# Eight output products per two steps for the last token pair, one accumulating DMA less, and output weights kept whole in DRAM

## The chip, the cores and the metric

The kernel runs on one core of one Trainium2 chip. The metric is the device time of one execution in microseconds (us). TensorE is called PE, its weight loads PEld, VectorE DVE, ScalarE ACT, GpSimd POOL and SyncE SP.

## The reference

```python
X = np.fft.rfft(x, axis=1)                      # x: 2 x 3008 x 256
Yr = Xr @ w_r - Xi @ w_i + b_r; Yi = Xr @ w_i + Xi @ w_r + b_i
Y = shrink(Yr, 0.01) + 1j * shrink(Yi, 0.01)
t = np.fft.irfft(Y, n=3008, axis=1).reshape(6016, 256)
h = t @ moe_w_in                                # 256 -> 2048
t = (h * clip(h + 3, 0, 6) / 6) @ moe_w_out     # 2048 -> 256
g, v = t @ moe2_w_gate, t @ moe2_w_val          # 256 -> 1536 each
out = (silu(g) * v) @ moe2_w_out                # 1536 -> 256
```

Everything is float32. A product of two float32 matrices is made of three fast matmuls: each operand is split into a high part and a rest (`hi`, `lo`), and low x high, high x high and high x low are added in one PSUM bank. "A product" below is such a group of three matmuls of a 128x128 weight block with up to 512 columns of tokens.

## The kernel before, in words

The 6016 tokens, kept transposed, form six **pairs** of two equal blocks: five pairs with 512 tokens per block and a last one with 448 (`pairs`, `halves`, L530 and L779). Three stages follow each other: the Fourier layer, the first feed-forward layer (`quad1`, L1003) and the second feed-forward layer, which the change touches (`quad`, L1280, and `last`, L1372). While `quad1` runs, `Convert2.steps` (L707) turns the float64 weights of the second layer into float32 parts, step by step, and writes one tile `Wd[f]` in DRAM for each of the 12 blocks f of 128 hidden units.

**A step of the second layer** is one pair p and one f: 72 steps. Its 2x2 block product (two token blocks, gate and value) is made with seven products in place of eight (`multiply`, numbers 1, 2, 7, 6, 4, 5 in the step and 3 in the next one), in the banks P, T and Q. P holds products 1, 6, 5 and 3 one after another; each partial result is copied out or added by ACT or DVE before the next product is added to it. P changes between two banks from step to step. Each step applies Silu twice (L1352, L1367) and multiplies gate and value (`times2`).

**The output products.** For two steps (f = 2k and 2k + 1) the output too is a 2x2 block product with seven products in place of eight. That needs sums of hidden units (`units`, four per k: T1 to T4, in SBUF) and of output weights (`out_sums`, `out_parts`, in the first pair). Three products of each k are made at once (`live`, into the banks `acc`); one of them takes T1, the other two sums that are ready in the next step. The other four wait (`later`): they are made in the steps of the **next** pair, two products per step, into one bank D. D begins with a copy of the first `acc` (`begin`, L1150), and `phase` reads it after steps 2, 5, 8 and 11. For them `part2` (L1140) splits units of two k at a time, 1024 columns on ACT (L1145) and DVE (L137), and `ask` (L1128) loads their weights (`chunk` from `Vd`). The last pair has no next pair: `last` makes its 24 waiting products, the last product 3 and two `live` products after all steps.

**Sums of units.** In an odd step T1 is added to T3 (L1306, `add_apart`: an accumulating DMA that POOL issues at L1254); T2 += T1 of the k before is a DVE instruction (`add_up`, L1251); T2 += T4 is another accumulating DMA. In the next even step DVE adds T2 to T3. Each instruction waits for the one whose result it reads.

**Weights.** Four slots hold the weights of a step: 14 blocks for the seven products and 2 or 4 output blocks, 1024 or 1152 KB per fetch (`fetch`, L854), issued on SP two steps ahead. A slot is free once the step after its own has used its output blocks. In the first pair `ask_out` (L1210) loads output weights for `out_sums`: as `Wd` holds them only as high part and rest, SP loads the one and POOL adds the other by an accumulating DMA. `out_parts` (L1238) writes the summed weights to `Vd` (512 KB) and `Wd`; in an odd step of the first pair SP meets those two writes, then the fetch of the odd step, then that of the next even step.

The order on each engine is the order of the calls; nothing reorders them (`manual_schedule`). Each queue works in order, and an instruction that waits holds up what is behind it.

Of the kernel before, what the change touches and what calls it, by code (L numbers as in the profile page):

```python
# [10 lines left out]
F32 = mybir.dt.float32  # L11
# [3 lines left out]
AF = mybir.ActivationFunctionType  # L15
# [67 lines left out]
def fourier_moe_kernel(ctx: ExitStack, tc: tile.TileContext, x, lin, bias, w1, w2, fwd1, inv2, fwd2,  # L83
# [17 lines left out]
    def one_bank(i, shape, name):  # L101
        return ps.tile(shape, F32, tag=f"pp{i % 5}", name=name, bufs=1)
# [593 lines left out]
    class Convert2(Convert):  # L696
# [10 lines left out]
        def steps(self):  # L707
            n = len(self.pieces)
            for i in range(4):
                self.load(i)  # L710
            yield
            self.scale(0)
            yield
            for i in range(n + 1):
                if i < n:
                    self.shift(i)
                if i > 0:
                    self.sign(i - 1, self.full_of(i - 1))
# [24 lines left out]
                yield  # L743

# [109 lines left out]
    def fetch(q):  # L854
        if q < len(stream):
            assert stream[q] in ready, (q, stream[q])
            slot[q] = free.pop(0)
            src = (Sd, Wd)[stream[q][0] - 1][stream[q][1]]
            c = src.shape[1] // 128
            if stream[q][0] == 2 and (stream[q][1] % 2 == 0 or q < len(quads1) + KF2):  # L860
                c = 16
            nc.sync.dma_start(slot[q][:, :c].bitcast(F32).rearrange("p a b -> p (a b)"), src[:, : c * 128])

    def side(k=1):
        for _ in range(k):
# [283 lines left out]

    def begin(p):  # L1150
        n = halves[p]
        D = C[p, 3] = C[p, 0] = one_bank(spot[0], [128, BLK], "D")
        a = acc.pop((p, 1))
        nc.scalar.copy(D[:, :n], a[:, :n])  # L1154
        c = C[p, "one"] = take("one")
        nc.scalar.copy(c[:, :n], a[:, :n])

    def later(p, i, half):
        m, kk = divmod(i, 3)
        n = halves[p]  # L1160
        (hi, lo), w = mid[p, i], mid[p, i, "w"]
        o = C[p, 3 * (m == 3)]
        wh, wl = w[:, 2 * half], w[:, 2 * half + 1]
        o, xh, xl = pairwise(o[:, :n]), woven(hi[:, half]), woven(lo[:, half])
        start = (p, "end") in C and i == 9 and not half
        nc.tensor.matmul(o, wl, xh, start=start, stop=False, skip_group_check=not start)  # L1166
        nc.tensor.matmul(o, wh, xh, start=False, stop=False, skip_group_check=not start)  # L1167
        nc.tensor.matmul(o, wh, xl, start=False, stop=True, skip_group_check=not start)

    def send_out(p, e, t, c, send=nc.sync):  # L1170
        n = halves[p]
# [2 lines left out]

    def phase(p, m):
        n = halves[p]
        D, one, three = C[p, 0][:, :n], C[p, "one"][:, :n], C[p, "three"][:, :n]
        if m == 0:
            nc.vector.tensor_tensor(out=one, in0=D, in1=one, op=ALU.subtract)
        elif m == 1:  # L1180
            nc.vector.tensor_tensor(out=three, in0=D, in1=three, op=ALU.add)
            send_out(p, 0, 1, three)
        elif m == 2:
            c = take("short")[:, :n]
            nc.scalar.copy(c, D)
            send_out(p, 1, 1, c)
            if (p, "end") in C:
                nc.vector.tensor_tensor(out=one, in0=D, in1=one, op=ALU.subtract)
        elif (p, "end") in C:
            nc.vector.tensor_tensor(out=one, in0=C[p, 3][:, :n], in1=one, op=ALU.add)  # L1190
            send_out(p, 1, 0, one)
# [46 lines left out]
    def out_parts(k):  # L1238
        g = G.pop(k)
        t = cv.tile([128, 4, 2, 128], F32R, tag="full", name="parts", bufs=2)  # L1240
        f = fourth[k] = cv.tile([128, 2, 128], F32R, tag="s4", name="s4", bufs=1)
        nc.scalar.copy(t[:, :, 0], g[:, :4])
        nc.scalar.copy(f[:, 0], g[:, 4])
        low(t[:, :, 1], g[:, :4], t[:, :, 0])
        low(f[:, 1], g[:, 4], f[:, 0])
        nc.sync.dma_start(Vd[:, :, k], t.bitcast(F32).rearrange("p m i c -> p m (i c)"))
        nc.sync.dma_start(Wd[2 * k + 1][:, 16 * 128 :], f.bitcast(F32).rearrange("p i c -> p (i c)"))

    def add_up(p, k, to, x):
        o = U(p, to, k)  # L1250
# [29 lines left out]
    def quad(q, before):  # L1280
# [84 lines left out]
        times2(U(p, ("T1", "T4")[odd], k), h0[:, :n], Q[:, :n], -1 if odd else 1)  # L1365
        todo.send()
        nc.scalar.activation(h1[:, :n], h1[:, :n], AF.Silu)  # L1367
        if f == NF - 1:
            begin(p)
        return p, k, odd, P, h1, product, n  # L1370

    def last(before):  # L1372
        p, k = before[:2]
        w = slot[F0 + len(quads2) - 1]
        order = (0, 1, 2, 3, 4, 5, 9, 6, 7, 8, 10, 11)
        C[p, "end"] = True
        C[p, 3] = one_bank(spot[0] + 4, [128, BLK], "E")

        def both(at):
            for half in range(2):  # L1380
                later(p, order[at], half)
            if at + 2 < 12:
                ask(p, order[at + 2])

        both(0)
        upper(before)
        part2(p, 1)
        x2 = halve(p, k, "T4")
        both(1)
        x3 = halve(p, k, "T2")  # L1390
        add_up(p, k, "T3", "T2")
        add_up(p, k, "T2", "T1")
        add_apart(p, k, "T4", "T2")
        part2(p, 2)
        live(p, 2, k, w[:, 14:16], x2)
        both(2)
        live(p, 3, k, w[:, 16:18], x3)
        corner(p)
        third(p)
        phase(p, 0)  # L1400
        part2(p, 3)
        for at in range(3, 12):
            both(at)
            if at + 1 < 12:
                part2(p, order[at + 1])
            if order[at] in (5, 8, 11):
                phase(p, order[at] // 3)

    lay_out()
    ask_out(0)  # L1410
# [2 lines left out]
    for q in range(len(quads2)):  # L1413
        if quads2[q][1] == 0 and quads2[q][0] + 1 < len(pairs):
            p = quads2[q][0] + 1
            todo.steps = iter(operands(len(pairs) + p, p, from_dram(len(pairs) + p, p)))
        before = quad(q, before)
    last(before)
    assert not pending


# [58 lines left out]
```

## Time and profile before

| | us |
|---|---|
| median of 3 runs (1171.15 to 1174.17) | 1174.11 |
| the profiled execution | 1175.45 |
| its span, first to last instruction | 1173.3 |

| engine | busy us, share of the span |
|---|---|
| PE | 1120.2 (95%) |
| PEld | 975.2 (83%) |
| DVE | 985.4 (84%) |
| ACT | 820.3 (70%) |
| POOL | 121.9 (10%) |

Mean granted TensorE clock: 0.985. Busy time is the time in which at least one instruction of the engine runs. Matmuls overlap in the trace: one of 512 columns is shown with 0.38 us, but the next begins sooner. In a timeline row the first number is the start, the second the duration; the bracket at the end tells how long the engine was idle before and what ended that. In a row of waits stand the total, the number of waits and the longest one. In a row of windows stand the stretch, its length, the busy time of PE, PEld, DVE, ACT and POOL (in brackets how many instructions), the granted clock, the DMA share and GB/s. The second layer runs from about 590 us on.

### The profile page before, as it was taken

Reading aid. Unit: us, or ns where it says so; the run is one execution under the profiler, and the core shown is the slowest. Engines: PE = TensorE matmul, PEld = TensorE weight load, DVE = VectorE, ACT = ScalarE, POOL = GpSimd, SP = SyncE. Lnnn points to the kernel's source line nnn. Section 1 sums busy time; section 2 is a strip of 40 time slices with the busy share of each in tenths; the row PEclk is TensorE's granted clock in tenths of the full one; section 3 lists DMA queues with packets and bytes.
Section 4 is the critical chain, followed back from the end, with each engine's and each line's share of the span. In section 5 each row is a group of like instructions: output and inputs, shape, how many; then the busy total and the mean of one; then the engine's idle time right before and its main releaser. Section 6 shows DMA issues by size and latency. Waiting matters only on the chain.

```text
span 1173.3 us, 20145 instructions
## 1 busy us (share of the span) xinstructions
PE 1120.2 (95%) x7362; PEld 975.2 (83%) x7362; DVE 985.4 (84%) x1720; ACT 820.3 (70%) x1506; POOL 121.9 (10%) x153
## 2 busy tenths in 40 slices
PE   8999999999999999999998788999999998999996
PEld 8999888788888888888997566887887887887885
DVE  6888888999999999999986676987887987887775
ACT  4777666787787888877876565676676776676573
POOL 3000018000000000000012211111111111111110
PEclk9999999999999999999999898999999999999998
DMA  7757337754645645645557878788688789679764
GB/s 299 283 178 230 95 96 240 259 195 163 210 157 173 227 162 168 225 144 179 194 144 211 247 233 269 219 279 276 196 272 280 221 244 310 188 242 289 229 176 131
DMA packets 94058, 250.32 MB, mean 213 GB/s; under 512 B 8836, under 2 KB 37796, under 8 KB 82504
## 3 DMA queue, kind: packets, MB, share of 16 engines
q1 hardware_dynamic: 78448, 222.61, 54.4%
q0 software_dynamic: 15360, 26.35, 11.8%
q8 instruction: 58, 0.95, 0.3%
q14 instruction: 40, 0.33, 0.1%
q10 hardware_dynamic: 152, 0.08, 0.0%
HBM read 186.48 MB, written 44.04 MB: 196 GB/s over the span
## 4 chain that ended last, share of the span: by engine, by line
PE 49%; issue 31%; DVE 7%; DMA 5%; POOL 4%; ACT 3%; ACTq 0%; POOLq 0%; DVEq 0%
PE acc L132 6%; PE acc L134 6%; PE acc L133 6%; POOL units L1254 4%; PE P L940 3%; PE P L942 3%; PE P L941 3%; DMA units<-units 2%; PE p L461 2%; PE p L367 2%; PE Tb L940 2%; PE Tb L941 1%; PE Tb L942 1%; PE p L417 1%; DVE r L988 1%
## 5 line engine op out<-in xcount | busy, mean ns | idle before, releaser
L617 ACT CAST gated<-r 128x512 fp32r<-128x512 f32 (+1 forms) x160 | 98.1, 613 | 64.7 <-DVE r L988 63.1
L1352 ACT ACTIVATE hv<-hv 128x512 f32<-128x512 f32 (+1 forms) x72 | 44.7, 621 | 127.6 <-DVE hv L1351 127.6
L137 DVE TENSOR_TENSOR gated<-r,gated 128x512 fp32r<-128x512 f32 (+1 forms) x160 | 108.0, 675 | 24.0 <-ACT gated L617 19.5
L132 PE MATMUL acc<-gated,w_o 128*128 128x512 f32 (+1 forms) x320 | 120.4, 376 | 0.0
L133 PE MATMUL acc<-gated,w_o 128*128 128x512 f32 (+1 forms) x320 | 119.6, 374 | 0.0
L134 PE MATMUL acc<-gated,w_o 128*128 128x512 f32 (+1 forms) x320 | 119.6, 374 | 0.0
L1254 POOL DMA_DIRECT2D units<-units x72 | 65.2, 1063 | 420.9 <-DVE hv L137 393.5
L940 PE MATMUL P<-xo,slot 128*128 128x512 f32 (+1 forms) x240 | 91.6, 382 | 5.4 <-DMA slot<-Wd 2.1
L984 ACT ACTIVATE r<-hold,consts 128x512 f32<-128x512 f32 (+1 forms) x120 | 85.5, 712 | 13.9 <-DVE hold L992 11.8
L942 PE MATMUL P<-xo,slot 128*128 128x512 f32 (+1 forms) x240 | 89.3, 372 | 0.0
L941 PE MATMUL P<-xo,slot 128*128 128x512 f32 (+1 forms) x240 | 89.3, 372 | 0.0
L988 DVE SCALAR_TENSOR_TENSOR r<-r,hold 128x512 f32<-128x512 f32 (+1 forms) x120 | 80.9, 674 | 2.6 <-ACT r L984 1.6
L1145 ACT CAST parts<-units 128x1024 fp32r<-128x1024 f32 (+1 forms) x72 | 74.2, 1032 | 5.2 <-PE D L1167 5.0
L1166 PE MATMUL D<-parts,chunk 128*128 128x512 f32 (+1 forms) x138 | 55.0, 399 | 17.6 <-ACT D L1154 7.3
L1270 ACT CAST live<-units 128x512 fp32r<-128x512 f32 (+1 forms) x108 | 63.7, 608 | 11.1 <-DVE units L1258 10.7
L132 PEld LDWEIGHTS acc<-gated,w_o 128*128 128x128 f32 x320 | 60.5, 189 | 7.0
L134 PEld LDWEIGHTS acc<-gated,w_o 128*128 128x128 f32 x320 | 60.5, 189 | 6.9
L133 PEld LDWEIGHTS acc<-gated,w_o 128*128 128x128 f32 x320 | 60.5, 189 | 6.7
L1251 DVE TENSOR_TENSOR units<-units 128x512 f32<-128x512 f32 (+1 forms) x72 | 48.6, 674 | 17.8 <-DMA units<-units 17.8
L137 DVE TENSOR_TENSOR parts<-units,parts 128x1024 fp32r<-128x1024 f32 (+1 forms) x36 | 43.3, 1202 | 21.9 <-ACT parts L1145 21.8
L1216 POOL DMA_DIRECT2D hv<-Wd x12 | 14.8, 1638 | 446.8 <-DMA hv<-Wd 419.1
L940 PEld LDWEIGHTS P<-xo,slot 128*128 128x128 f32 x240 | 45.4, 189 | 16.8 <-DVE hv L1364 4.5
(249 smaller groups left out, 3419.3 us busy)
## 6 DMA issues: line engine op xcount, KB each, us to landing
slot<-Wd SPq DMA_DIRECT2D x42, 1024.0 KB
slot<-Sd SPq DMA_DIRECT2D x40, 896.0 KB
slot<-Wd SPq DMA_DIRECT2D x30, 1152.0 KB
chunk<-Vd SPq DMA_DIRECT2D x72, 256.0 KB
st<-in_w SPq DMA_DIRECT2D x68, 256.0 KB
units<-units POOLq DMA_DIRECT2D x60, 256.0 KB, 6.3
Wd<-slot SPq DMA_DIRECT2D x12, 1152.0 KB
m<-in_fwd SPq DMA_DIRECT2D x12, 512.0 KB
```

The costliest lines, as they stand in the source:

```text
L132: nc.tensor.matmul(o, wl, xh, start=start, stop=False)
L133: nc.tensor.matmul(o, wh, xh, start=False, stop=False)
L134: nc.tensor.matmul(o, wh, xl, start=False, stop=stop)
L137: nc.vector.tensor_tensor(out=o, in0=full, in1=hi.bitcast(F32), op=ALU.subtract)
L617: nc.scalar.copy(hi[:, :n], g[:, :n])
L940: nc.tensor.matmul(o, wl, hi, start=start, stop=False, skip_group_check=not start)
L941: nc.tensor.matmul(o, wh, lo, start=False, stop=False, skip_group_check=not start)
L942: nc.tensor.matmul(o, wh, hi, start=False, stop=True, skip_group_check=not start)
L984: nc.scalar.activation(r[:, :n], x[:, :n], AF.Relu, bias=three)
L988: nc.vector.scalar_tensor_tensor(out=r[:, :n], in0=r[:, :n], scalar=6.0, in1=x[:, :n], op0=ALU.min, op1=ALU.mult)
L1145: nc.scalar.copy(hi, t[:, :, :n])
L1254: nc.gpsimd.dma_start(U(p, to, k), U(p, x, k), accum_op=ALU.add)
```

## The change

- The last pair makes its output products directly, all eight for two steps (four per step), and none of them waits: `last` goes, and `plain` takes the place of `quad` for f = 1 to 11 of the last pair and is called once more for the end. It still makes the waiting products of the pair before. Its P stays in one bank, as the other one holds the fourth output sum. The two values of a step are kept in two spots (`own`), and `share` multiplies those of the step before.
- T3 += T1 in odd steps is a DVE instruction (`add_up`) in place of an accumulating DMA; for the last pair no unit sums are made at all. 30 of 72 accumulating DMAs of L1254 are left.
- In the step f = 11 the copy from the first `acc` to D is issued after L1338's copy and so ahead of both Silu instructions; its second copy (`one`) stays behind them.
- The conversion also writes the full output weights to a new DRAM tile `Od`; `Wd[f]` has 20 blocks in place of 18 and is written by two DMAs. `ask_out` is one load of 256 KB from `Od`, without an accumulating DMA.
- A fetch of the last pair is two DMAs (16 blocks, and 2 blocks from the end of `Wd[f]`).

```diff
-    Wd = [dram.tile([128, SLOT * 128], F32, name=f"Wd{f}") for f in range(KF2)]
+    Wd = [dram.tile([128, 20 * 128], F32, name=f"Wd{f}") for f in range(KF2)]
+    Od = [dram.tile([128, 4, 128], F32, name=f"Od{k}") for k in range(KF2 // 2)]
...
                 O = full.pop((f, 2))
+                nc.sync.dma_start(Od[f // 2][:, f % 2 * 2 : f % 2 * 2 + 2], O)
...
-                nc.sync.dma_start(Wd[f], t.bitcast(F32).rearrange("p a b -> p (a b)"))
+                nc.sync.dma_start(Wd[f][:, : 16 * 128], t[:, : 16 * 128])
+                nc.sync.dma_start(Wd[f][:, 18 * 128 :], t[:, 16 * 128 :])
...
+            if stream[q][0] == 2 and p == len(pairs) - 1:
+                nc.sync.dma_start(to[:, 16 * 128 :], src[:, 18 * 128 :])
...
     def begin(p):
         n = halves[p]
-        D = C[p, 3] = C[p, 0] = one_bank(spot[0], [128, BLK], "D")
+        D = C[p, "D"] = one_bank(spot[0], [128, BLK], "D")
         a = acc.pop((p, 1))
+        C[p, "one"] = take("one")
         nc.scalar.copy(D[:, :n], a[:, :n])
-        c = C[p, "one"] = take("one")
-        nc.scalar.copy(c[:, :n], a[:, :n])
+        return lambda: nc.scalar.copy(C[p, "one"][:, :n], a[:, :n])
...
     def ask_out(k):
         F[k] = take("outs").rearrange("p (a b) -> p a b", b=128)
-        for i in range(2):
-            t = F[k][:, 2 * i : 2 * i + 2]
-            w = Wd[2 * k + i][:, 14 * 128 :].rearrange("p (e h c) -> p e h c", e=2, h=2)
-            nc.sync.dma_start(t, w[:, :, 0])
-            nc.gpsimd.dma_start(t, w[:, :, 1], accum_op=ALU.add)
+        nc.sync.dma_start(F[k], Od[k])
...
             x1 = halve(p, k, "T1")
-            add_apart(p, k, "T1", "T3")
+            add_up(p, k, "T1", "T3")
...
             fetch(F0 + q + ASK)
+            if f == NF - 1:
+                then = begin(p)
...
         if f == NF - 1:
-            begin(p)
+            then()
...
-    def last(before):
...
+    def plain(q, before):
...
+        if p is not None:
+            fetch(F0 + q + ASK)
...
+        last(Pb, 3)
+        s1 = take("own")
+        times2(s1[:, :n], hb[:, :n], Pb[:, :n], 1)
+        if p is not None:
+            later(old, i, 0)
+            later(old, i, 1)
+        x0 = parted(state["own"])
+        if p is None:
+            x1 = parted(s1)
+            for t, x in enumerate((x0, x1)):
+                for e in range(2):
+                    share(t, e, x)
...
+        product(P, 1, start=True)
+        nc.scalar.copy(Q[:, :n], P[:, :n])
+        x1 = parted(s1)
+        if i % 3 == 2:
+            phase(old, i // 3)
+        product(T, 7, start=True)
...
+        share(0, 0, x0)
+        product(Q, 2)
+        product(P, 6)
+        if i + 1 < NF:
+            part2(old, i + 1)
...
+        share(0, 1, x0)
+        product(T, 4)
...
+        share(1, 0, x1)
+        product(P, 5)
+        h1 = take("h")
+        nc.vector.tensor_tensor(out=h1[:, :n], in0=P[:, :n], in1=c7, op=ALU.add)
+        share(1, 1, x1)
+        free.append(slot.pop(F0 + q - 1))
+        state["own"] = take("own")
+        times2(state["own"][:, :n], h0[:, :n], Q[:, :n], 1)
+        nc.scalar.activation(h1[:, :n], h1[:, :n], AF.Silu)
```

`share` is one product (three matmuls) of a step's value, split by `parted` (a copy on ACT, a subtraction on DVE), with an output block of the slot. In the last call the fourth sum is copied out in two halves, one by DVE and SP's queue, one by ACT and ACT's queue.

## Rows read from the trace of the kernel before

**Rows 1.** Windows: one of the first layer, pairs 1, 4 and 5, the end.

```profile
225.00:590.00 365.00, 363.43 (x2375) 319.14 (x2374) 341.60 (x635) 292.14 (x519) 0.00 (x0) 1.00 0.53 182
...
722.50:807.50 85.00, 82.55 (x380) 71.16 (x380) 73.04 (x106) 59.75 (x102) 10.41 (x12) 1.00 0.83 256
...
981.30:1068.80 87.50, 84.23 (x381) 72.44 (x380) 72.45 (x106) 58.95 (x102) 10.44 (x12) 0.98 0.78 248
1068.80:1142.10 73.30, 69.01 (x339) 63.67 (x337) 55.59 (x85) 46.42 (x84) 10.47 (x12) 0.98 0.74 221
1142.10:1173.30 31.20, 20.47 (x81) 16.26 (x81) 18.14 (x22) 13.40 (x19) 0.86 (x1) 0.86 0.48 138
```

**Rows 2.** Windows: two stretches at half clock; two-step cycles of the first pair.

```profile
652.70:656.10 3.40, 3.16 (x7) 2.08 (x8) 3.27 (x9) 1.70 (x4) 0.00 (x0) 0.50 0.98 332
...
1144.20:1151.00 6.80, 5.76 (x17) 4.57 (x15) 4.89 (x8) 2.10 (x4) 0.00 (x0) 0.50 0.37 116
630.90:644.70 13.80, 11.55 (x53) 9.44 (x52) 11.10 (x22) 8.98 (x19) 3.49 (x4) 1.00 0.73 239
...
694.20:707.80 13.60, 11.14 (x49) 8.46 (x47) 11.81 (x22) 8.95 (x19) 1.74 (x2) 1.00 0.76 244
```

**Rows 3.** Waits of PE from 615 to 720 us (the first pair).

```profile
PE P L940 <- DMA slot<-Wd: 10.9, 5, 3.0
...
PE D L1166 <- DMA chunk<-Vd: 5.2, 1, 5.2
```

**Rows 4.** Waits from 720 to 1142 us (pairs 1 to 5).

```profile
DVE parts L137 <- ACT parts L1145: 20.2, 29, 2.0
...
DVE units L1251 <- DMA units<-units: 11.9, 5, 2.9
...
PE D L1166 <- ACT D L1154: 5.5, 4, 1.4
...
PE P L940 <- DVE hv L1364: 3.5, 5, 0.7
...
PE D L1166 <- DVE sums L1179: 2.3, 4, 0.8
PE P L940 <- DMA slot<-Wd: 2.1, 1, 2.1
PE D L1168 <- DVE lows L137: 2.1, 5, 0.4
```

**Rows 5.** DMA queues from 643 to 653 us, and one kind of issue.

```profile
q1 hardware_dynamic: 862, 2.08, 62.8%
q0 software_dynamic: 759, 0.67, 43.2%
...
units<-units POOLq DMA_DIRECT2D x2, 256.0 KB, 11.1
```

**Rows 6.** Timeline: DVE's additions L1251 in steps 1 and 2 of pair 3.

```profile
897.68 0.69 DVE L1251 TENSOR_TENSOR units<-units 128x512 f32<-128x512 f32 x1
...
907.59 0.69 DVE L1251 TENSOR_TENSOR units<-units 128x512 f32<-128x512 f32 x1 [2.52 <-DMA units<-units]
```

**Rows 7.** Timeline: matmuls of the last pair, its last step, and the end.

```profile
1124.77 0.38 PE L1166 MATMUL D<-parts,chunk 128*128 128x512 f32 x1
...
1125.41 0.35 PE L940 MATMUL Tb<-xo,slot 128*128 128x448 f32 x1
...
1125.60 0.35 PE L941 MATMUL Tb<-xo,slot 128*128 128x448 f32 x1
...
1140.97 0.35 PE L942 MATMUL P<-xo,slot 128*128 128x448 f32 x1
...
1141.47 0.61 DVE L1364 TENSOR_TENSOR hv<-P,cc 128x448 f32<-128x448 f32 x1
...
1142.12 0.58 ACT L1367 ACTIVATE hv<-hv 128x448 f32<-128x448 f32 x1
...
1169.72 0.62 DVE L1190 TENSOR_TENSOR sums<-E,sums 128x448 f32<-128x448 f32 x1 [1.12 <-PE E L1168]
```

More of the change, by code (lines that the diff above doesn't have):

```diff
@@ L858, in fetch @@
             src = (Sd, Wd)[stream[q][0] - 1][stream[q][1]]
[L859 to L862, printed above, removed]
+            c, p = src.shape[1] // 128, (q - len(quads1)) // KF2
+            if stream[q][0] == 2:
+                c = 18 if stream[q][1] % 2 and 0 < p < len(pairs) - 1 else 16
+            to = slot[q].bitcast(F32).rearrange("p a b -> p (a b)")
+            nc.sync.dma_start(to[:, : c * 128], src[:, : c * 128])
+            if stream[q][0] == 2 and p == len(pairs) - 1:
+                nc.sync.dma_start(to[:, 16 * 128 :], src[:, 18 * 128 :])
     def side(k=1):
@@ L1161, in later @@
         (hi, lo), w = mid[p, i], mid[p, i, "w"]
-        o = C[p, 3 * (m == 3)]
+        o = C[p, "D"]
         wh, wl = w[:, 2 * half], w[:, 2 * half + 1]
         o, xh, xl = pairwise(o[:, :n]), woven(hi[:, half]), woven(lo[:, half])
[L1165 to L1168, printed above, removed]
+        nc.tensor.matmul(o, wl, xh, start=False, stop=False, skip_group_check=True)
+        nc.tensor.matmul(o, wh, xh, start=False, stop=False, skip_group_check=True)
+        nc.tensor.matmul(o, wh, xl, start=False, stop=True, skip_group_check=True)
     def send_out(p, e, t, c, send=nc.sync):
@@ L1364, in quad @@
         nc.vector.tensor_tensor(out=h1[:, :n], in0=P[:, :n], in1=c7, op=ALU.add)
-        times2(U(p, ("T1", "T4")[odd], k), h0[:, :n], Q[:, :n], -1 if odd else 1)
+        if q == len(quads2) - NF:
+            d = home.pop()
+            spots["own"] = [d[:, 0], d[:, 1]]
+            state["own"] = take("own")
+        times2(state["own"][:, :n] if p == len(pairs) - 1 else U(p, ("T1", "T4")[odd], k), h0[:, :n], Q[:, :n], -1 if odd else 1)
         todo.send()
@@ L1368, in quad, with share, where, parted @@
         if f == NF - 1:
-            begin(p)
+            then()
         return p, k, odd, P, h1, product, n
-    def last(before):
[L1373 to L1407, printed above, removed]
+    def plain(q, before):
+        p, f = quads2[q] if q < len(quads2) else (None, None)
+        pb, old, i = len(pairs) - 1, len(pairs) - 2, f
+        n = halves[pb]
+        _, _, _, Pb, hb, last, _ = before
+        w = slot[F0 + q - 1]
+        if p is not None:
+            fetch(F0 + q + ASK)
+        def share(t, e, x):
+            if q == len(quads2) - NF + 1:
+                where = acc_bank
+                if t and e:
+                    def where(shape, name):
+                        return bank_p(F0 + q)
+                acc[t, e] = where([128, BLK], f"acc{t}{e}")
+            mm3(acc[t, e][:, :n], w[:, 14 + 2 * e], w[:, 15 + 2 * e], *x, q == len(quads2) - NF + 1, p is None)
+        def parted(x):
+            hi, lo = (take(c)[:, :n] for c in ("hi", "lo"))
+            nc.scalar.copy(hi, x[:, :n])
+            low(lo, x[:, :n], hi)
+            return hi, lo
+        last(Pb, 3)
[10 more added lines that the diff above has]
+                    share(t, e, x)
+                    a = acc.pop((t, e))
+                    if t and e:
+                        for o, c, copy, send in ((take("short"), slice(0, n // 2), nc.vector.tensor_copy, nc.sync),
+                                                 (take("h"), slice(n // 2, n), nc.scalar.copy, nc.scalar)):
+                            copy(o[:, c], a[:, c])
+                            at = pairs[pb][0] + n
+                            send.dma_start(out[e * 128 : e * 128 + 128, at + c.start : at + c.stop], o[:, c])
+                    else:
+                        o = take("short")
+                        (nc.vector.tensor_copy if e else nc.scalar.copy)(o[:, :n], a[:, :n])
+                        send_out(pb, e, t, o)
+            return None
+        k, odd = divmod(f, 2)
+        if f == 1:
+            add_up(old, NK - 1, "T2", "T1")
+            add_apart(old, NK - 1, "T4", "T2")
+        P, T, Q = Pb, one_bank(spot[0] + 3, [128, BLK], "Tb"), bank_q([128, BLK], "Q")
+        P = one_bank(spot[0] + 1 + (F0 + len(quads2) - NF) % 2, [128, BLK], "P")
+        product = multiply(B[len(pairs) + p], F0 + q, n)
+        product(P, 1, start=True)
[4 more added lines that the diff above has]
+        product(T, 7, start=True)
+        c7 = ring2["c"]()[:, :n]
+        nc.scalar.copy(c7, T[:, :n])
+        share(0, 0, x0)
[3 more added lines that the diff above has]
+            part2(old, i + 1)
+        if i + 2 < NF:
+            ask(old, i + 2)
+        cu = ring2["c"]()[:, :n]
+        nc.scalar.copy(cu, P[:, :n])
+        share(0, 1, x0)
+        product(T, 4)
+        h0 = take("h")
+        nc.vector.tensor_tensor(out=h0[:, :n], in0=T[:, :n], in1=cu, op=ALU.add)
+        nc.scalar.activation(h0[:, :n], h0[:, :n], AF.Silu)
+        share(1, 0, x1)
[4 more added lines that the diff above has]
+        free.append(slot.pop(F0 + q - 1))
+        state["own"] = take("own")
+        times2(state["own"][:, :n], h0[:, :n], Q[:, :n], 1)
+        nc.scalar.activation(h1[:, :n], h1[:, :n], AF.Silu)
+        return p, k, odd, P, h1, product, n
@@ L1416, in fourier_moe_kernel @@
             todo.steps = iter(operands(len(pairs) + p, p, from_dram(len(pairs) + p, p)))
-        before = quad(q, before)
-    last(before)
+        before = (plain if q > len(quads2) - NF else quad)(q, before)
+    plain(len(quads2), before)
     assert not pending
```

10 lines of the change are left out of this document (3 added, 7 removed).

## The prediction, made before the changed kernel was run

> **What bounds the kernel now.** I read the windows by stage first. In the first layer PE is busy 363.4 of 365.0 us at full clock [rows 1], so what the change adds to the conversion there (24 more small DMAs on SP) is paid only if PE has to wait for it. In the second layer PE is nearly full too: pairs 1 to 4 take 85.0 us in the first and 87.5 us in the last of four windows, 346.3 us together. A matmul of 512 columns starts (1125.41 - 1124.77) / 3 = 0.213 us after the one before, one of 448 columns 0.19 us [rows 7]. A pair has 378 matmuls, 80.6 us at 0.213. So pairs 1 to 4 lose about 6 us each, and that is all that can be won in them. Two stretches lose much more: the first pair, and the end, where 81 matmuls (15.4 us at 0.19) take 31.2 us [rows 1].
>
> The waits tell why. In the first pair PE waits five times for a slot, 10.9 us, and once for a chunk, 5.2 us [rows 3]; in the later pairs mainly for D's copy, for DVE's subtraction on D and what DVE does behind it [rows 4]. The granted clock falls from full to half (2.4 to 1.2 GHz) in eight stretches of 3.4 to 6.8 us, each beginning during or shortly behind a wait of PE [rows 2]; at half clock half of such a stretch is lost.
>
> **The change part by part.** The sum is made against the profiled execution, 1175.45 us, which is 1.3 us above the median 1174.11.
>
> *First pair: less DMA work ahead of the slots.* In a stretch in which a slot is late, the queues run full: the accumulating DMAs (q0) hold 43.2% of 10 us of the 16 DMA engines, the plain ones 62.8% [rows 5]. The q0 share, 4.3 us, is one accumulation for `ask_out` and two of units; the change takes the first away and one of the two, so about 2/3 of it, 2.9 us. Against that, DVE's new T3 addition comes ahead of the subtraction that the `Vd` write waits for, and the fetches stand behind this write on SP: all of them come one DVE instruction later, 0.6 us (0.69 us shown in rows 6, the next one starting 0.6 us on). The gain for a slot is so about 2.3 us, and the waits are 2.2 us on average (10.9 / 5): most of them go. With three half-clock stretches of 3.4 us (1.7 us lost in each) this is up to 10.9 + 5.1 = 16 us; below, nothing comes if the bursts stay. DVE is busy 11.1 and 11.8 us of a two-step cycle of 13.8 and 13.6 us [rows 2] and gets 0.6 more, so a cycle can't go below about 12.4 us; five cycles now take 707.8 - 630.9 = 76.9 us, and 5 x 12.4 = 62 leaves 15. I take **-11 us**, as some slots will still be a little late, with -2 and -16 as ends. The chunk wait (5.2 us and a half-clock stretch of 6.8 us) has the same queue ahead of it with 1 accumulation less: **-1**, ends 0 and -8. The one load from `Od` has two steps of cover.
>
> *T3 on DVE, pairs 1 to 4.* Once per pair DVE waits for the accumulation that adds T1 to T3: 2.52 us in the row, 11.9 us in five waits [rows 4, 6]. What follows on PE are the waits for DVE at D: 2.3 + 2.1 + 3.5 = 7.9 us, about 6.4 of it in these four pairs, and two half-clock stretches behind them (3.5 us lost). With the addition on DVE itself nobody waits for that DMA; T4's, which stays, is read only steps later. The new instruction costs 0.6 us per odd step, but in the 29 odd steps DVE waits 20.2 us for ACT's cast in `part2` right behind that place, 0.7 us each [rows 4]. That hides it; without this cover it would be 24 steps x 0.6 = 14 us. **-9 us**, ends -11 and +5.
>
> First the row: one such DMA of 256 KB lands 11.1 us after its issue in a busy stretch [rows 5]. The Trainium skill, "DMA: Bandwidth & Descriptors", section "Anatomy of one DMA", gives about 2.0 us and bytes over 436 GB/s, an estimate of 2.6 us here. By that nothing would have waited for it and this term would be 0; the trace disagrees, since it counts a DMA with the queues to itself.
>
> *D's copy ahead of Silu.* PE waits 5.5 us in four waits for the copy L1154 [rows 4]; it now stands behind both Silu instructions. Moved ahead of them, it follows L1338's copy, where ACT waits for DVE anyway before the first Silu. Late next would be the chunk or `part2`'s subtraction, both a step old by then. **-5 us**, ends -5.5 and -2.
>
> *Last pair, steps.* Until the end of its steps it makes 16 own `live` products now, 44 after: 28 x 3 x 0.19 = 16 us more on PE. A new step has 33 matmuls of 448 and 6 of 512 columns: 6.3 + 1.3 = 7.55 us. A wait is new: product 3 adds to P, which h1's addition has to read first, and only one output product (0.57 us) stands between. In the last step now that addition ends 1141.47 + 0.61 - 1140.97 = 1.11 us after the last matmul of product 5 starts [rows 7]; PE is free again 0.19 + 0.57 = 0.76 us after it, and so waits 0.4 us per step. Product 1 starts in the same bank behind `times2`, but six matmuls of `later` (1.3 us) cover that. Eleven steps of 7.95 us are 87.5 us against 73.3 now [rows 1]: **+14 us**; that 73.3 holds a slot wait of 2.1 us with a half-clock stretch and the pair's share of the waits at D, which I let go, as slots are now asked two full steps ahead and no unit DMA is left. Ends: +11 with no wait at P, +20 with one of a DVE instruction more per step. The second DMA of a fetch (128 KB) has the same two steps of cover.
>
> *Last pair, end.* Now 31.2 us from the last Silu to the end [rows 1]. After: product 3 0.8, `times2` 0.7, copy 0.6, subtraction 0.7, the remaining output products 1.5, the half copies 0.5, and from the copy's end to the landed store 3.0 as now (1173.3 - 1169.72 - 0.62): 7.8 us. **-23 us**, ends -24 and -20. The pair as a whole gains 9.
>
> *Conversion, all else*: 0; `Od`'s write comes a step ahead of the `Wd` write for which SP waits there today.
>
> **Sum**: -11 - 1 - 9 - 5 + 14 - 23 = -35, so 1140.4 against the profiled execution, and **1139 us** as a median. The unfavourable ends of all terms together (-2, 0, +5, -2, +20, -20) give 1175, the favourable ones (-16, -8, -11, -5.5, +11, -24) 1121.
>
> **The rivals.**
>
> *The slots stay late (chance 0.2).* The `Vd` write and two fetches still leave SP in one burst, 0.6 us later. For: the plain queue alone fills 62.8% of that stretch [rows 5]. Against: what goes is more than the mean wait. It leaves the first pair as it is: 1139 + 12 = 1151.
>
> *The last pair gives nothing (0.12).* PE is the fullest engine and gets 18 matmuls more in all, and its steps hang on one bank P: steps of 9 us, 99 in place of 87.5 us, cancel the rest of the gain: 1139 + 9 to 12 = 1149. Beside it: the Trainium skill, "Perfetto Trace Analysis", section "Identifying the Most-Contended Engine", has one relieve the fullest engine first. By that rule the pair would lose the 18 x 0.19 = 3.4 us that it adds; the window of the end, with PE busy 20.5 of 31.2 us [rows 1], speaks against it.
>
> *DVE's addition is not covered (0.1).* Then its 14 us come back: 1153.
>
> *Slower than before (0.04).* In the last pair everything runs through P in turn: product 1, copy, product 6, copy, product 5, addition, product 3, multiplication. If each link also waited for what its engine has queued ahead (ACT's cast of 1.0 us, DVE's subtraction of 1.2 us), a step would be 12 us, and eleven of them 44 us more: 1183. It decides from 11.2 us per step, 3.2 more than I count. Against: now ACT and DVE are busy 46.4 and 55.6 of 73.3 us [rows 1], 4 to 5 us per step.
>
> *The change doesn't do it (0.04).* Waits at D come from elsewhere and the clock falls as before: within 0.3% of 1174.
>
> **How the numbers follow.** Forecast with its own spread: 0.5, 1130 to 1147. Slots late 0.2, last pair 0.12, DVE 0.1, no change 0.04, slower 0.04. From 1126 to 1156 the range takes in the first four cases; some of the upper side with two of them at once is left out. About 0.3% (3.5 us) is what a measurement of this kernel tells from no change. Faster 0.92, within 0.04, slower 0.04.
>
> **What would show it.** In the profile after: no accumulating DMA from `Wd`, 30 of units; in the first pair slot waits under 4 us in all and at most one half-clock stretch ahead of 710 us; no wait of L1251 for a DMA; no wait of PE for L1154; pairs 1 to 4 in 82 to 84 us each; last-pair steps of 8 us with waits of 0.4 us before product 3; 8 us from the last Silu to the end. Steps of the last pair above 9 us, slot waits of 10 us, or DVE's L1351 and L1364 ahead of many waits of PE in pairs 1 to 4 would make the prediction wrong.

## The result, and the profile after

The changed kernel takes **1140.55 us** (median of 4 runs, 1137.94 to 1141.14); the kernel before took 1174.14 us beside it (1171.15 to 1174.82). The ratio is 0.9714 with a 95% interval of 0.9692 to 0.9737. The prediction, 1139 us with a range of 1126 to 1156, holds. The profiled execution of the changed kernel took 1137.94 us, 2.6 us below its median, while that of before was 1.3 us above its own; so the spans below differ by 37.1 us (1173.3 to 1136.2), the medians by 33.6.

From the profile page of the changed kernel: busy time and instructions by engine, the granted clock in 40 slices, two groups of DVE and POOL, and the DMA issues of units with their time to landing.

```profile
PE 1107.2 (97%) x7380; PEld 970.1 (85%) x7380; DVE 985.4 (87%) x1729; ACT 812.4 (71%) x1499; POOL 70.3 (6%) x99
...
PEclk9999999999999999999999998999999999999999
...
L1251 POOL DMA_DIRECT2D units<-units x30 | 26.2, 873 | 811.4 <-DVE parts L138 434.9
...
L1248 DVE TENSOR_TENSOR units<-units 128x512 f32<-128x512 f32 x90 | 59.5, 687 | 1.0
...
units<-units POOLq DMA_DIRECT2D x30, 256.0 KB, 7.5
```

In the second layer POOL issues 30 accumulations of units and no other DMA. Ahead of its 90 additions DVE stands idle for 1.0 us in all, where from 720 to 1142 us alone it had waited 11.9 us for such DMAs [rows 4]. Next, the windows of the changed kernel, cut at the second Silu of the same steps as in the sum: the first pair's five two-step cycles, step 0 of pair 1, pairs 1 to 4, the last pair's eleven steps, the end. The columns are those of [rows 1].

```profile
629.60:696.90 67.30, 58.28 (x253) 45.65 (x251) 59.66 (x111) 44.66 (x89) 4.41 (x5) 1.00 0.66 235
696.90:710.40 13.50, 10.28 (x37) 8.60 (x38) 7.21 (x12) 5.78 (x11) 0.00 (x0) 0.75 0.80 278
710.40:1039.90 329.50, 327.44 (x1509) 283.79 (x1508) 307.04 (x445) 237.47 (x405) 20.90 (x24) 1.00 0.76 244
1039.90:1127.00 87.10, 85.47 (x429) 79.80 (x427) 52.69 (x81) 49.77 (x89) 0.87 (x1) 1.00 0.49 169
1127.00:1136.20 9.20, 3.64 (x15) 2.59 (x15) 3.30 (x6) 3.12 (x6) 0.00 (x0) 0.94 0.27 100
```

Their lengths against the same stretches of before:

| stretch | before, us | after, us | difference | forecast |
|---|---|---|---|---|
| up to step 1 of the first pair | 630.9 | 629.6 | -1.3 | 0 |
| first pair, five cycles | 76.9 | 67.3 | -9.6 | -11 |
| step 0 of pair 1 (chunk) | 14.7 | 13.5 | -1.2 | -1 |
| pairs 1 to 4 | 346.3 | 329.5 | -16.8 | -14 (T3 -9, copy -5) |
| last pair, eleven steps | 73.3 | 87.1 | +13.8 | +14 |
| end | 31.2 | 9.2 | -22.0 | -23 |

The first row is no effect: in the runs below this stretch takes 629.1 to 632.4 us. In pairs 1 to 4 PE is now busy 327.4 of 329.5 us. Ahead of the last microseconds one half-clock stretch is left, where the page's row of the clock shows an 8: in step 0 of pair 1 (mean clock 0.75). The waits of PE from 600 to 705 us in the changed kernel (engine, bank and line, what it waited for; total, times, longest):

```profile
PE D L1172 <- DMA chunk<-Vd: 5.0, 1, 5.0
PE P L947 <- DMA slot<-Wd: 3.4, 5, 0.8
PE Q L947 <- ACT Q L1296: 3.1, 6, 0.6
PE Tb L947 <- DVE hv L1350: 1.2, 4, 0.3
```

The slots are late by 3.4 us in five waits, where it was 10.9 [rows 3]; the chunk is as late as before. PE's last matmul ahead of the wait for the chunk and its first one behind it, in the kernel before and then in the changed kernel (start, duration, in brackets the idle time before and what ended it):

```profile
706.35 0.38 PE L942 MATMUL P<-xo,slot 128*128 128x512 f32 x1
711.95 0.76 PE L1166 MATMUL D<-parts,chunk 128*128 128x512 f32 x1 [5.22 <-DMA chunk<-Vd]
```

```profile
694.77 0.38 PE L949 MATMUL P<-xo,slot 128*128 128x512 f32 x1
700.12 0.76 PE L1172 MATMUL D<-parts,chunk 128*128 128x512 f32 x1 [4.97 <-DMA chunk<-Vd]
```

Then the waits of PE's weight loads from 1040 to 1128 us, and rows of the timeline of the end (ACT's copy of the third output block, the last matmul of the fourth and its two half copies):

```profile
PEld P L947 <- DVE hv L1456: 5.5, 11, 0.5
```

```profile
1130.81 0.53 ACT L1421 COPY hv<-acc 128x448 f32<-128x448 f32 x1 [0.60 <-PE acc L135]
...
1130.99 0.35 PE L135 MATMUL P<-lows,slot 128*128 128x448 f32 x1
1132.32 0.39 DVE L1416 COPY sums<-P 128x224 f32<-128x224 f32 x1 [1.46 <-DMA out_t<-sums]
...
1132.75 0.34 ACT L1416 COPY hv<-P 128x224 f32<-128x224 f32 x1 [1.41 <-DVE sums L1416]
```

Ahead of product 3 the weight loads wait 0.5 us at P for DVE's addition, in ten of the eleven steps and in the call at the end (0.4 was forecast for PE). These ten steps take 7.95 to 7.98 us; the first takes 7.5. At the end the last block isn't copied by two halves beside each other: DVE, idle for 1.46 us, begins its half when an earlier store out of the same spot has ended, 1.33 us after the last matmul of the block starts, and ACT's half follows behind DVE's.

### The profile page after: what moved, and what is told of

It reads as the page before. It is cut to its first block, busy times and chain, and to the rows that moved or that the text cites. A ratio compares the mean times of both kernels' runs of the same rounds, so it can differ in the third digit from the quotient of the medians.

```text
span 1136.2 us, 20001 instructions
## 1 busy us (share of the span) xinstructions
PE 1107.2 (97%) x7380; PEld 970.1 (85%) x7380; DVE 985.4 (87%) x1729; ACT 812.4 (71%) x1499; POOL 70.3 (6%) x99
## 4 chain that ended last, share of the span: by engine, by line
PE 77%; DVE 12%; DMA 5%; ACT 3%; issue 2%; POOL 0%; SPq 0%; DVEq 0%; ACTq 0%; POOLq 0%
PE P L947 7%; PE acc L133 7%; PE acc L135 7%; PE acc L134 7%; PE P L949 7%; PE P L948 7%; DMA slot<-Wd 4%; PE Tb L947 3%; PE Tb L948 3%; PE Tb L949 3%; DVE r L995 2%; PE D L1172 2%; PE D L1173 2%; PE D L1174 2%; DVE gated L138 2%
## 5 line engine op out<-in xcount | busy, mean ns | idle before, releaser
L1351 ACT ACTIVATE hv<-hv 128x512 f32<-128x512 f32 (+1 forms) x61 | 38.4, 630 | 96.5 <-DVE hv L1350 96.5
L1251 POOL DMA_DIRECT2D units<-units x30 | 26.2, 873 | 811.4 <-DVE parts L138 434.9
L1152 ACT CAST parts<-units 128x1024 fp32r<-128x1024 f32 x60 | 63.1, 1052 | 0.0
L1248 DVE TENSOR_TENSOR units<-units 128x512 f32<-128x512 f32 x90 | 59.5, 687 | 1.0
L947 PEld LDWEIGHTS P<-xo,slot 128*128 128x128 f32 x240 | 45.3, 189 | 17.5 <-DVE hv L1456 5.5
L1267 ACT CAST live<-units 128x512 fp32r<-128x512 f32 x90 | 53.6, 616 | 5.1 <-DVE units L1255 4.8
L1172 PE MATMUL D<-parts,chunk 128*128 128x512 f32 x120 | 46.1, 384 | 5.0 <-DMA chunk<-Vd 5.0
L948 PEld LDWEIGHTS P<-xo,slot 128*128 128x128 f32 x240 | 45.4, 189 | 4.4
L949 PEld LDWEIGHTS P<-xo,slot 128*128 128x128 f32 x240 | 45.4, 189 | 4.3
```

What stands on the lines that cost most here:

```text
L947: nc.tensor.matmul(o, wl, hi, start=start, stop=False, skip_group_check=not start)
L948: nc.tensor.matmul(o, wh, lo, start=False, stop=False, skip_group_check=not start)
L949: nc.tensor.matmul(o, wh, hi, start=False, stop=True, skip_group_check=not start)
L1152: nc.scalar.copy(hi, t[:, :, :n])
L1172: nc.tensor.matmul(o, wl, xh, start=False, stop=False, skip_group_check=True)
```

## The experiments

All medians are of runs in rounds with the kernel before on the same chip. "The changed kernel" is the one above; its second run comes first. The four kernels from "One output product moved" to "The three edits together" ran on another chip than this second run. Of these four, only the three edits together have a ratio whose interval lies clear of the changed kernel's (0.9692 to 0.9737); the single edits are judged by their stretches.

**The changed kernel again.**

> The changed kernel itself, for the difference of the others to it on one chip: 1138 to 1142 us; first pair's five cycles 66.5 to 69 us, pairs 1 to 4 in 328 to 332 us, the eleven last-pair steps 87.1 us, 9.2 us to the end.

Measured: 1140.23 us (1139.76 to 1140.83), ratio 0.9742 (0.9711 to 0.9773). First pair 68.0 us, pairs 1 to 4 329.5, the eleven steps 87.1, end 9.2. So a difference of 0.7 us in the first pair is no effect.

**T3's addition by DMA again.**

```diff
-            add_up(p, k, "T1", "T3")
+            add_apart(p, k, "T1", "T3")
```

> The changed kernel with T3 += T1 as an accumulating DMA again (60 of them in place of 30); all else stays. Theory (a DMA that DVE waits for once per pair, and a share of the queues in the first pair): in pairs 1 to 4 DVE waits 2 to 3 us per pair for it, PE 1.5 to 2 us behind that, at least one half-clock stretch returns, 7 to 10 us together; in the first pair slot waits grow from 3.4 us to 6 to 9 us. 1149 to 1154 us. Rival (the gain of pairs 1 to 4 is all D's copy, and the first pair is bound by DVE, which is relieved here): 1139 to 1142 us.

Measured: 1151.92 us (1150.21 to 1154.2), ratio 0.9831 (0.9769 to 0.9893). Pairs 1 to 4 take 340.1 us, 10.6 more. Waits of DVE from 720 to 1040 us, first in this run, then in the changed kernel (which waits for no DMA there):

```profile
DVE parts L138 <- ACT parts L1152: 12.7, 21, 0.9
DVE units L1248 <- DMA units<-units: 10.2, 4, 3.0
```

```profile
DVE parts L138 <- ACT parts L1152: 0.9, 5, 0.2
```

and PE's over the whole of pairs 1 to 4, first in this run (712.8 to 1052.9 us), then in the changed kernel (710.4 to 1039.9):

```profile
PE P L947 <- DVE hv L1363: 4.0, 5, 1.1
PE P L947 <- DMA slot<-Wd: 3.3, 5, 1.3
PE D L1174 <- DVE lows L138: 1.7, 4, 0.4
PE D L1172 <- DVE sums L1185: 1.4, 3, 0.8
```

```profile
PE P L947 <- DVE hv L1363: 1.2, 1, 1.2
PE P L947 <- DMA slot<-Wd: 0.6, 1, 0.6
```

The wait of DVE for the DMA returns, and with it PE's three kinds of waits for DVE. The cover is visible too: with the addition on DVE, its waits for ACT's cast shrink from 12.7 to 0.9 us, 11.8 of the 14 us that 24 additions cost. The first pair takes 68.0 us, unchanged, though its slot waits grow from 3.4 us (4.1 in the second profile) to 7.7 us. DVE is busy 56.2 us there in place of 59.7; that its shorter work gives back what the slots lose fits this, but no run shows it by itself.

**D's copy behind the Silus again.**

```diff
-            if f == NF - 1:
-                then = begin(p)
...
-            then()
+            begin(p)()
```

> The changed kernel with both copies of begin behind the second Silu again; all else stays. Theory: PE waits 1.35 us for the copy to D at the start of pairs 2 to 5 (in pair 1 the chunk wait covers it), 5 us in all: 1145 to 1147 us. Rival (without the DMA wait behind it DVE and ACT take the delay up within the next steps): under 2 us, 1140 to 1142.5 us.

Measured: 1144.44 us (1143.61 to 1146.0), ratio 0.9764 (0.9714 to 0.9815); by the median 3.9 us slower, between the two expectations. The trace of this run, PE from 720 to 1048 us, decides:

```profile
PE D L1172 <- ACT D L1162: 6.8, 4, 1.8
```

Four waits, none of which the changed kernel has; pairs 1 to 4 take 334.9 us, 5.4 more. The copy's place is worth 5 us.

**Output weights added up by DMA again** (two loads and two accumulations from `Wd` in place of the load from `Od`).

```diff
-        nc.sync.dma_start(F[k], Od[k])
+        for i in range(2):
...
+            nc.sync.dma_start(t, w[:, :, 0])
+            nc.gpsimd.dma_start(t, w[:, :, 1], accum_op=ALU.add)
```

> The changed kernel with the output weights of the first pair put together from Wd by 12 loads and 12 accumulating DMAs of 128 KB again, Od written but not read; all else stays. Theory (these DMAs stand in the queues ahead of the slots): slot waits of the first pair 3.4 us now, 7 to 10 us here, with one or two half-clock stretches: 1145 to 1150 us. Rival (the first pair's two-step cycle of 13.4 us is set by DVE, and the T3 addition was the DMA that mattered): 1140 to 1142.5 us.

Measured: 1142.99 us (1141.87 to 1144.17), ratio 0.9751 (0.97 to 0.9801). The first pair takes 70.1 us: 2.8 more than in one profile of the changed kernel, 2.1 more than in the other. Slot waits are 6.1 us, no half clock. Alone it is worth 2 to 3 us, less than the theory had.

**All three undone: the last pair alone is new.**

> The last three edits together: what is left of the change is the last pair by eight products without waiting ones, and the layout of Wd. Theory: the last pair alone gives 9 us against the kernel before (14 more in its steps, 23 less at the end): 1163 to 1167 us, the first pair and pairs 1 to 4 as before the change. Rival (the last pair gives nothing by itself, as its steps need the lighter queues): 1172 to 1176 us.

Measured: 1168.85 us (1165.84 to 1173.15, 10 runs), ratio 0.9973 (0.9943 to 1.0004): by the time not told from before. By stretches: last pair 87.1 + 8.9 = 96.0 us against 104.5 before, -8.5; pairs 1 to 4 349.8 us, 3.5 more; first pair 80.8 us, 3.9 more than before. The profiled execution is the slowest of the ten, 4.3 us above their median, so these 3.5 and 3.9 us may be its own. The window of these five cycles, and PE's waits from 600 to 725 us:

```profile
630.40:711.20 80.80, 62.50 (x253) 49.30 (x251) 56.55 (x106) 44.25 (x89) 16.32 (x16) 0.92 0.77 223
```

```profile
PE P L947 <- DMA slot<-Wd: 10.5, 5, 3.0
...
PE Tb L947 <- DVE hv L1352: 4.7, 1, 4.7
```

The late slots and the half clock (mean 0.92) are back, and one long wait for DVE. With one relief alone the first pair takes 68 or 70 us, with both undone 80.8 (76.9 in the kernel before): the two don't add up. Only with both loads on the queue does a slot come 3.0 us late, here as before [rows 3], and does half clock appear in these cycles; with one of them the longest slot wait is 1.8 us.

**The old last pair alone, the rest as changed.**

> The changed kernel with the old last pair alone: its steps with five output products and waiting products, and the old end; the rest as changed. It is the counterpart of the kernel in which only the last pair is new. Theory (the last pair's gain is its own: eleven steps grow by 14 us, the end shrinks by 22 us): eleven steps of 71 to 73.5 us in all and 31 us of end, so 1137.9 + 6 to 9 for the profiled execution, 1145 to 1149 us by the median; if DVE's addition helps the last pair's old steps as it helps pairs 1 to 4 (2.6 us per pair), the low end of this. Rival (the last pair gains nothing once the other parts are in: the steps of the old last pair fall to 66 us or less): 1139 to 1142 us.

Measured: 1145.49 us (1143.97 to 1146.43), ratio 0.9785 (0.9752 to 0.9818), 5.3 above the changed kernel on this chip. The old pair's steps, as a window:

```profile
1042.10:1111.90 69.80, 69.41 (x352) 65.19 (x352) 58.81 (x91) 47.12 (x86) 5.22 (x6) 1.00 0.70 225
```

They take 69.8 us where they took 73.3 [rows 1] and 71 at least was expected, with PE busy 69.4; the end takes 30.9. So the new pair costs 17.3 in its steps and gives 21.7 at the end: 4.4 us by the trace, where it is 8.5 without the other parts. Of the 4.1 us between, 3.5 lie in the old pair's steps, from which the other parts take 1.5 us of PE's waits (3.5 us before, 2.0 here) and the half-clock stretch.

**One output product moved** behind product 5 in the last pair's steps.

```diff
-        share(1, 0, x1)
         product(P, 5)
...
+        share(1, 0, x1)
         share(1, 1, x1)
```

> One line is moved in the changed kernel: in a step of the last pair the first output product of the second half stands behind product 5, so that six matmuls in place of three lie between product 5 and product 3 of the next step, which needs the bank P that DVE reads. Theory (what is left of the last-pair step's wait is only this DVE addition, and 0.57 us more of matmuls covers it): the eleven waits of 0.5 us before product 3 go, and no other takes their place; steps of about 7.5 us in place of 7.95, the eleven 83 us in place of 87.1, the rest as in the changed kernel, 1135 to 1138 us. Rival (the step is a chain through the one bank P: product 5 now waits for ACT's copy of product 6, which the moved product had covered): the wait moves ahead of product 5, the steps stay at 7.9 us or grow, 1139.5 to 1143 us.

Measured: 1135.42 us (1133.84 to 1136.29), ratio 0.9689 (0.9656 to 0.9722). The weight loads' waits from 1040 to 1126 us:

```profile
PEld P L947 <- DVE hv L1363: 1.6, 1, 1.6
PEld acc L133 <- ACT live L1396: 0.8, 1, 0.8
PEld P L947 <- ACT cc L1447: 0.3, 1, 0.3
PEld P L947 <- DVE hv L1455: 0.3, 1, 0.3
```

The first line lies ahead of the eleven steps, the second behind them. The repeated wait is gone (one of the eleven is left, at 0.3) and most steps take 7.54 us, all of them 82.8: 4.3 us won. 7.55 was the prediction's count of a step's matmuls, and PE is busy in all of the 82.8 us, so PE sets these steps now. The rival's wait for ACT's copy shows once, at 0.3 us.

**The chunk's load ahead of the last write of units.**

```diff
+        if k == NK - 1:
+            ask(0, 0)
         nc.sync.dma_start(Vd[:, :, k], t.bitcast(F32).rearrange("p m i c -> p m (i c)"))
...
-                    ask(0, 0)
                     ask(0, 1)
```

> The changed kernel with one issue moved: the load of the first chunk of the waiting products is queued on SP ahead of the last write of units in place of behind it. Theory (the chunk that comes 5.0 us late at the start of the second pair is late by its place in SP's queue): the wait falls to 2 us or less, the half-clock stretch of 698 to 705 us, which begins beside it, is gone or shorter; step (1,0) takes 9 to 11.5 us in place of 13.5; 1135 to 1138.5 us. Rival (the chunk waits for the write of the weights that it reads, or for its buffer, not for its place in the queue): wait and half clock stay, 1139.5 to 1142 us.

Measured: 1137.7 us (1135.9 to 1138.3), ratio 0.9709 (0.9681 to 0.9736). Windows 696 to 700 and 700 to 706 us of this run, PE's waits from 600 to 712, and waits of SP's queue from 685 to 703 us with the issue of the moved load:

```profile
696.00:700.00 4.00, 1.64 (x7) 1.05 (x6) 3.90 (x7) 1.67 (x5) 0.87 (x1) 1.00 0.48 93
700.00:706.00 6.00, 5.56 (x26) 4.92 (x27) 4.49 (x7) 4.11 (x8) 0.00 (x0) 1.00 1.03 329
```

```profile
PE P L947 <- DMA slot<-Wd: 5.6, 6, 1.4
...
PE D L1172 <- DMA chunk<-Vd: 2.8, 1, 2.8
```

```profile
SPq L1144 <- DVE s L138: 10.3, 1, 10.3
```

```profile
697.14 0.32 SPq L1144 DMA_DIRECT2D chunk<-Vd  x1
```

The place in the queue was part of the cause: the wait falls from 5.0 to 2.8 us (2 or less was expected), the clock stays at full in this execution, and the step takes 8.9 us in place of 13.5. What is left of the wait has another source: the moved load is itself held until 697.14 us by a subtraction of DVE, which holds the write in the changed kernel. So it is issued about when PE's last matmul ahead of the wait starts (697.26), and the first matmul on it starts at 700.44. Not all is kept: the slot behind it is late by 1.4 us in the next step (8.2 in place of 6.6). Over both steps 2.9 us remain; the ratio (0.9709 against 0.9714) doesn't show them.

**The last block copied whole by ACT** into a free spot.

```diff
-                        for o, c, copy, send in ((take("short"), slice(0, n // 2), nc.vector.tensor_copy, nc.sync),
-                                                 (take("h"), slice(n // 2, n), nc.scalar.copy, nc.scalar)):
-                            copy(o[:, c], a[:, c])
...
+                        o = take("h")
+                        nc.scalar.copy(o[:, :n], a[:, :n])
+                        send_out(pb, e, t, o)
```

> The changed kernel with another end: the fourth output block is copied whole by ACT into a spot that no store is using, and stored by SP in one piece, in place of two halves, DVE's and ACT's. Theory (DVE's half waits 1.5 us for the spot's earlier store and ACT's half runs behind DVE's, not beside it): the copy begins 1.4 us earlier and takes 0.3 us longer; from the last Silu to the end 7.9 to 8.4 us in place of 9.2; 1138.5 to 1140.5 us by the median, which may not tell it from the changed kernel, so the trace decides. Rival (ACT's copy is held by something else, such as its own queue, or the store of the whole block takes longer than the halves did): 9 us or more to the end.

Measured: 1138.25 us (1137.16 to 1140.84), ratio 0.9719 (0.969 to 0.9748). The end of this run's timeline:

```profile
1132.70 0.35 PE L135 MATMUL P<-lows,slot 128*128 128x448 f32 x1
1133.14 0.53 ACT L1415 COPY hv<-P 128x448 f32<-128x448 f32 x1
```

The copy begins 0.44 us after the last matmul starts; from the last Silu (1128.7) to the end of the span (1136.6) it takes 7.9 us in place of 9.2. The median doesn't tell it from the changed kernel, the trace does.

**The three edits together.**

> The three edits together (the last pair's output product moved, the chunk's load ahead of the write, the end by one copy). Theory (three places that do not meet): the gains add up, 4.4 + 3 to 5 + 1.2 us, so 1129 to 1133 us and a ratio to the kernel before of 0.962 to 0.966; it beats both kernels. Rival (one of the three waits is only moved): 1133.5 to 1138 us.

Measured: **1131.99 us** (1131.6 to 1132.24), ratio 0.9662 (0.9636 to 0.9688). It beats both kernels. Steps 82.8 us, end 8.0. The chunk's step takes 10.5 us, not 8.9: with a wait of 2.7 us the clock does fall in this profile:

```profile
700.00:706.00 6.00, 5.32 (x17) 4.41 (x18) 3.71 (x6) 3.28 (x7) 0.00 (x0) 0.72 1.03 326
```

**POOL adds T3 in the first pair.**

```diff
-        nc.vector.tensor_tensor(out=o, in0=o, in1=U(p, x, k), op=ALU.add)
+        engine = nc.gpsimd if p == 0 and x == "T3" else nc.vector
+        engine.tensor_tensor(out=o, in0=o, in1=U(p, x, k), op=ALU.add)
```

> The changed kernel with one operation moved in the first pair alone: the six additions of T3 to T1 run on POOL in place of DVE; all other pairs as they are. Theory (the first pair's two-step cycle of 13.4 us is DVE's own work, about 13 us of it, since DVE builds operands for the next pair there too): without 0.69 us of DVE the cycle falls to 12.6 to 13.0 us, the five cycles from 67.3 to 63 to 65.5 us, and the waits of PE for DVE's and ACT's results there shrink; 1136 to 1139 us. Rival (the cycle is set by when the slots come, or POOL's addition is slow and DVE waits for it): the five cycles stay at 66.5 us or more, slot waits grow; 1140 to 1144 us.

Measured: 1141.54 us (1140.37 to 1144.23), ratio 0.9754 (0.9725 to 0.9784). The five cycles take 70.0 us, 2.0 to 2.7 more. The theory's gain did not come. Groups of POOL and DVE in this run from 640 to 695 us (busy, mean ns):

```profile
L1249 POOL TENSOR_TENSOR units<-units 128x512 f32<-128x512 f32 x4 | 6.6, 1650 | 46.4 <-DVE hv L138 46.4
...
L138 DVE TENSOR_TENSOR parts<-outs,parts 128x512 fp32r<-128x512 f32 x4 | 7.1, 1766 | 0.0
```

Three rows of its timeline:

```profile
653.68 0.68 DVE L1249 TENSOR_TENSOR units<-units 128x512 f32<-128x512 f32 x1
...
653.85 1.65 POOL L1249 TENSOR_TENSOR units<-units 128x512 f32<-128x512 f32 x1 [11.32 <-DVE hv L138]
...
654.28 1.76 DVE L138 TENSOR_TENSOR parts<-outs,parts 128x512 fp32r<-128x512 f32 x1
```

The same group in the changed kernel:

```profile
L138 DVE TENSOR_TENSOR parts<-outs,parts 128x512 fp32r<-128x512 f32 x5 | 3.4, 685 | 0.0
```

DVE's subtraction that starts during POOL's addition takes 1.77 us in place of 0.69. So DVE loses 1.08 us per cycle and saves 0.69, and the cycles grow by 0.4 to 0.5 us each, by what DVE's work grows (0.39). PE's waits for DVE at Tb grow from 1.2 to 2.6 us, its slot waits hardly (4.3 us, against 3.4 and 4.1 in the two profiles of the changed kernel). The edit failed as a relief, but speaks for DVE as what sets these cycles.

```profile
PE P L947 <- DMA slot<-Wd: 4.3, 5, 1.4
...
PE Tb L947 <- DVE hv L1351: 2.6, 4, 0.7
```

**The same on top of the three edits.**

> The kernel with the three edits together and POOL's addition in the first pair. Theory (DVE bounds the first pair): 2 to 4 us less than with the three edits alone, 1128 to 1130.5 us. Rival: no change from it, 1131 to 1134 us.

Measured: 1134.39 us (1132.8 to 1135.6), ratio 0.9689 (0.9662 to 0.9717): the first pair takes 69.8 us in place of 68.6, no gain, as the run before explains.

## Why the prediction was right, step by step

- **First pair, -11: measured -9.6.** Mechanism right, size 1.4 us too large: the slot waits fell from 10.9 to 3.4 us and the half-clock stretches went. The forecast came to 13.2 us per cycle and counted with "a cycle can't go below about 12.4 us", DVE's busy time and one instruction more. The cycles stand at 13.5 us (67.3 / 5), with DVE busy 59.7 of 67.3 us, so that floor wasn't reached; what holds them above it isn't shown. The runs speak for slots and DVE taking turns: less DVE work with later slots gave 68.0 (T3 by DMA), later slots alone 70.1, more DVE work 70.0. The step "2/3 of 4.3 us" treated the two accumulations as shares that add up; they don't: undone alone they cost at most 1 and 3 us, together 9 to 13.
- **Chunk, -1: measured -1.2, by luck.** The wait that the term was about fell by 0.2 us only, and the half-clock stretch behind it is 6.8 us long as before (698.2 to 705.0 us, mean clock 0.50). Some 0.7 us of the 1.2 come from where the stretch is cut: before the change the second Silu (707.80 us) stands 1.4 us behind the start of PE's last matmul ahead of the wait, after it (696.95) 2.2 us, and the first pair's stretch is longer by as much. The reason "the same queue ahead of it" is shown in part by the run that moved the load: two issues earlier, the wait fell by 2.2 us, and the rest stands behind DVE.
- **T3 and D's copy, -14 together: measured -16.8.** The undone parts cost 10.6 and 5.4 us, 16.0 in all, against forecasts of 9 and 5. The cover by ACT's cast was real (12.7 to 0.9 us). The term that was mis-sized is T3's. Undone, it brings 5.9 us of PE's waits for DVE (7.1 against 1.2), about the 6.4 that I had, but no half clock there; in its place come 2.7 us of slot waits (3.3 against 0.6), which the kernel before does not have in these pairs. PE is also busy 2.2 us longer (329.6 against 327.4 us in the windows of the two stretches).
- **Last pair's steps, +14: measured +13.8.** Ten steps of 7.95 to 7.98 us, 7.95 forecast, with the wait of 0.5 us at P; the first is shorter by the wait (7.5). But the step "I let go the pair's share of the waits at D" matters for what the last pair is worth: against old steps of 69.8 us the new ones cost 17.3. The pair's gain of 9 us holds next to the kernel before (8.5), and is 4.4 to 5.3 us once the other parts are in.
- **End, -23: measured -22.0.** The step "the half copies 0.5" failed: one half came after the other, behind a spot whose store had not ended. Of DVE's 1.46 us idle about 0.9 are this store's, since with a free spot the copy begins 0.44 us after the last matmul starts and here 1.33 us. The end with one copy takes 7.9 us; 7.8 was forecast.
- **The rule named with the rivals.** Optimizing the fullest engine first (the Trainium skill, "Perfetto Trace Analysis", section "Identifying the Most-Contended Engine") does not decide here. The section judges TensorE's headroom by the busy time of its weight loads or its share of peak, not by that of its matmuls; by the weight loads PE (83% of the span before) is no fuller than DVE (84%). 18 more matmuls paid, because they replaced a stretch in which PE was busy 20.5 of 31.2 us [rows 1].
- **The rivals.** Slots stay late: no, 3.4 us of waits. The last pair gives nothing: no, 4.4 to 8.5 us. DVE's addition uncovered: no. The chain through P: there, at 0.5 us per step; it needed 3.2 us more to decide. The 0.3% by which the prediction told a change from none is too fine: beside the run with T3 by DMA, 13 executions of the kernel before took 1165.5 to 1178.3 us.

What stays open: why the clock fell in one profile with a chunk wait of 2.7 us and not in the other with 2.8. It differs between executions of one kernel: with the chunk's load moved the mean granted clock was 1.0 in the profiled execution and 0.997 to 0.998 in the other three. Open too is whether, without DVE's share, the first pair's cycle would go below 13 us, as no run took work off DVE without loading the DMA queues or POOL.

## What to carry to other kernels

Parts that relieve the same wait need not add up: undo each alone and all together, and price the last one against what the others leave. Where a bank has to be read before its next matmul, count the matmuls between; one product moved gave 4.3 us over eleven steps. A buffer whose store is still under way is not free for the last copy.

## What the runs showed of the hardware

An addition of 128x512 f32 takes 0.69 us on DVE and 1.65 us on POOL, where DVE adds two SBUF operands in the first 0.5 us of it; POOL's time without that isn't shown. A DVE subtraction of two SBUF operands that starts during POOL's addition takes 1.77 us: it ends 0.54 us after POOL's addition (656.04 and 655.50 us), close to the 0.69 us that it takes alone. The Trainium skill, "Advanced Engine Details and Errata", section "GPSIMD Details", says that POOL shares a read and a write interface with DVE and conflicts with DVE instructions that have two SBUF inputs; these rows agree.

An accumulating DMA of 256 KB lands, by the median, 7.5 us after its issue where 30 of them run, and 5.6 us where 60 do (the profile pages of the changed kernel and of T3's run):

```profile
units<-units POOLq DMA_DIRECT2D x60, 256.0 KB, 5.6
```

The 60 include 30 at another place of the step, so this is no price of their number. Both stand far above the estimate of 2.6 us worked out from the Trainium skill, "DMA: Bandwidth & Descriptors", section "Anatomy of one DMA", whose sum has a fixed time and one for the bytes and none for other transfers.

ACT's copy of half of a PSUM bank began only 0.04 us after DVE's copy of the other half had ended, in the changed kernel's end. Its row names DVE's copy as what released it, and releasers are read from semaphores, so the program's own order makes it so; what the chip would do without that order no run shows. Two engines' copies out of one bank were not two at once here.
